# Split float32r products in place of one float32 product in the first transform step of the last two groups

## The chip, the cores and the metric

The kernel runs on one core of a Trainium2 chip. The metric is the device time of one launch in microseconds. Before the change, three runs took 2855.52, 2855.0 and 2850.59 us, a median of 2855.0.

The names of the engines: PE multiplies matrices (PEld is its loading of weights), DVE and ACT work on vectors, POOL is the fourth engine, SP issues most of the DMAs.

## The reference, cut to what matters

```python
X = np.fft.rfft(x, axis=1)                 # x: 8 batches, 3008 points, 256 channels
Yr = Xr @ w_r - Xi @ w_i + b_r
Yi = Xr @ w_i + Xi @ w_r + b_i
Yr = np.sign(Yr) * np.maximum(np.abs(Yr) - lam, 0.0)      # the same for Yi
y = np.fft.irfft(Yr + 1j * Yi, n=3008, axis=1)
gate = 1.0 / (1.0 + np.exp(-(y @ w_gate)))                # 256 -> 1536
out = (gate * (y @ w_val)) @ w_out                        # 1536 -> 256
```

3008 is 47 x 64. The forward transform is done as 47-point transforms over the rows of a batch (the "a" step), stored to DRAM, and then as 64-point transforms with twiddles (the "b" step). The changed products are those of the "a" step.

## The kernel before, in words

**Stages.** Eight batches are transformed in five groups of 1, 1, 2, 2 and 2 batches (`GROUPS`). Batches 0 and 1 and the "a" step of batches 2 and 3 are done in the first part, whose order is written by hand. From there on the main loop runs the gated feed-forward layer over columns of the output that are ready (`ffn[j]()`, 12 products of 512 columns into the banks pg and pv, and 6 into po for the unit two earlier). Beside it runs a list `side` with the transforms of the later groups: the "a" steps of group 3 (batches 4 and 5) merged with the rest of groups 1 and 2, and the "a" steps of group 4 (batches 6 and 7) merged with the rest of group 3. A unit of `side` is taken when the accumulated rate has paid its weight (the first entry of each pair); a step of "a" weighs 1.7. What is left of the program, a scheme with fewer products for the other columns, follows from about 1100 us.

**What sets the order.** Outside the parts under `manual_schedule`, the program's instructions are put in order by a scheduler that looks ahead: within each engine's queue it may put an instruction of a later unit ahead of one of an earlier unit. On the chip each engine then works through its queue in that order, and waits where an input or a buffer isn't free.

**A unit of "a"** (`step_a`, line 426) loads a tile two steps ahead (`load_a`), calls `fwd_a` (line 175) and stores the result (`store_a`). `fwd_a` makes two products of 94 x 512 elements by `fa_sb` (94 x 96) into banks named pa, straight from the loaded float32 tile `xf`, and ACT copies each bank back into `xf`. There are 2 groups of 2 batches of 8 such steps, 32 in all, with 64 products.

**A unit of the rest** (`step`, line 448) has three pieces for three different q: `fwd_b` (products pb, copy xsf, split into xsh and xsl), `mix` (18 products pm and pm3, the sums yt and ys, the soft threshold yc at lines 253 and 254, and the split into yh and yl) and `inv_b` (6 products pi, the copy vz). `inverse` adds products pia of the last inverse step. These products are float32r already, where their input is split into a high and a low part: high by high, high by low and low by high weights. pb and pia are float32.

**Buffers.** Banks pa, pb, pm, pm3, pi and pia share three PSUM buffers (`FFT_BANKS`). yt, ys and yc take turns in five buffers of the tag f2k (`NF2K`).

Of the kernel before, what the change touches and what calls it, by code (L numbers as in the profile page):

```python
# [10 lines left out]
F32R = mybir.dt.float32r  # L11
# [8 lines left out]
R2, R1 = 47, 64  # L20
NK2 = 24
NQ = 2 * NK2
# [7 lines left out]
NF2K, NR2K, NLD, NST, NBIG, NME, NVF, NVO, NHH, NSG, NYF = 5, 4, 3, 3, 5, 2, 3, 1, 3, 2, 2  # L30
# [9 lines left out]
def _r12(v):  # L40

    m, e = np.frexp(v)
    return np.ldexp(np.rint(m * 4096.0), e - 12)


def _split(v):
    hi = _r12(v)
    lo = _r12(v - hi)
    return hi.astype(np.float32), lo.astype(np.float32)


def _cs(num, den):

    num = np.asarray(num, np.int64) % den
    a = 2.0 * np.pi * num / den
    c, s = np.cos(a), np.sin(a)
    q = 4 * num
    c[(q == den) | (q == 3 * den)] = 0.0
    s[(num == 0) | (2 * num == den)] = 0.0
    return c, s  # L60


def _tables(seq):
    n2 = np.arange(R2)
    k2 = np.arange(NK2)
    c, s = _cs(n2[:, None] * k2[None, :], R2)
    fa = np.zeros((R2, 2, NK2, 2, 2))
    fb = np.zeros((NK2, 2, 2, 128))
    for j in range(2):
        fa[:, j, :, 0, j] = c  # L70
        fa[:, j, :, 1, j] = -s
        fb[:, 0, j, j:2 * R2:2] = c.T / seq
        fb[:, 1, j, j:2 * R2:2] = -s.T / seq
    fa = fa.reshape(2 * R2, 2 * NQ)
    fb = fb.reshape(2 * NQ, 128).astype(np.float32)
    n1 = np.arange(R1)
    k1 = np.arange(R1)
    mf = np.zeros((NK2, 128, 128), np.float32)
    mi = np.zeros((NK2, 128, 128), np.float32)
    mis = np.zeros((NK2, 128, 2, 128), np.float32)  # L80
    for q in range(NK2):
        k = q + R2 * k1
        c, s = _cs(n1[:, None] * k[None, :], seq)
        flip = np.where(k > seq // 2, -1.0, 1.0)
        m = np.zeros((2, R1, 2, R1))
        m[0, :, 0] = c
        m[1, :, 0] = s
        m[0, :, 1] = -s * flip
        m[1, :, 1] = c * flip
        w = np.full(R1, 2.0)  # L90
        if q == 0:
            w[k > seq // 2] = 0.0
            w[(k == 0) | (2 * k == seq)] = 1.0
        e = np.zeros((2, R1, 2, R1))
        e[0, :, 0] = (w * c).T
        e[1, :, 0] = (-w * flip * s).T
        if q:
            e[0, :, 1] = (w * s).T
            e[1, :, 1] = (w * flip * c).T
        mf[q] = m.reshape(128, 128)  # L100
        mi[q] = e.reshape(128, 128)
        mis[q, :, 0], mis[q, :, 1] = _split(e.reshape(128, 128))
    return {"mf": mf, "mi": mi, "mis": mis, "fa": fa.astype(np.float32), "fb": fb}


@with_exitstack
def tile_fft_mix_ffn(ctx: ExitStack, tc, x, w_r, w_i, b_r, b_i, w_one, w_out, mf, mi, mis, fa, fb, out):
    nc = tc.nc
    B, S, D = x.shape
    P = 128  # L110
# [11 lines left out]
    sub = nc.vector.tensor_sub  # L122
# [7 lines left out]
    cw = fft.enter_context(tc.tile_pool(name="cw", bufs=1))  # L130
    p2 = fft.enter_context(tc.tile_pool(name="p2", bufs=2))
# [4 lines left out]
    def bank(name, tag="fft", bufs=FFT_BANKS):  # L136
        return (psf if tag == "fft" else psl).tile([P, 512], F32, tag=tag, bufs=bufs, name=name)
# [6 lines left out]

    fa_sb = cw.tile([2 * R2, 2 * NQ], F32, name="fa_sb")
    nc.scalar.dma_start(fa_sb, fa)

    zd = [tc.dram_tile([NQ, R1, D], F32, name=f"zd{b}") for b in range(B)]
    vd = [tc.dram_tile([NQ, R1, D], F32, name=f"vd{b}") for b in range(B)]
# [7 lines left out]
    held = {}  # L157
# [6 lines left out]
    def load_a(b, h):  # L164
        xf = p0.tile([P, 4, D], F32, name="xf0", bufs=R1 // 8) if b == 0 else big("xf")
        for lo_, hi_ in ((0, 64), (64, 2 * R2)):
            nc.sync.dma_start(xf[lo_:hi_], xv[b, lo_:hi_, 4 * h:4 * h + 4])
        held["x", b, h] = xf

    def product_a(xi, az, copy):  # L170
        pa = bank("pa")[:2 * NQ]
        nc.tensor.matmul(pa, fa_sb, xi, start=True, stop=True)  # L172
        copy(az, pa.rearrange("p (h c) -> p h c", h=2))

    def fwd_a(b, h):

        xf = held["x", b, h]
        for i in range(2):
            at = slice(2 * i, 2 * i + 2)
            product_a(xf[:2 * R2, at], xf[:2 * NQ, at], nc.vector.tensor_copy if b < 2 and i else nc.scalar.copy)  # L180

    def store_a(b, h, queue=nc.sync):
        queue.dma_start(zv[b][:, 4 * h:4 * h + 4], held.pop(("x", b, h))[:2 * NQ])

    def load_half(b, h):
        xf = p2.tile([P, 2, D], F32, tag="ld", bufs=NLD, name="xfh")
        for lo_, hi_ in ((0, 64), (64, 2 * R2)):
            nc.sync.dma_start(xf[lo_:hi_], xv[b, lo_:hi_, 2 * h:2 * h + 2])
        held["xh", b, h] = xf
# [9 lines left out]
    def load_mf(q):  # L199
        t = p2.tile([P, 2, P], F32, name="mf_sb", bufs=NME)  # L200
        nc.sync.dma_start(t, mf[2 * q:2 * q + 2].rearrange("q p k -> p q k"))
        return t

    def load_mi(q, full):
        t = p2.tile([P, 2, 2, P], F32 if full else F32R, tag="mi_sb", bufs=NME, name="mi_sb")
        if full:
            t = t[:, :, 0]
            nc.sync.dma_start(t, mi[2 * q:2 * q + 2].rearrange("q p k -> p q k"))
        else:
            m = md[2 * q:2 * q + 2].rearrange("q p a k -> p q a k")  # L210
            if q in kept:
                nc.sync.dma_start(t.bitcast(F32), m)
            else:

                nc.gpsimd.dma_start(t, mis[2 * q:2 * q + 2].rearrange("q p a k -> p q a k"))
                nc.gpsimd.dma_start(m, t.bitcast(F32))
                kept.add(q)
        return t

    def load_b(b, q):  # L220
        zf = p2.tile([P, 2, D], F32, tag="ld", bufs=NLD, name="zf")
        nc.sync.dma_start(zf, zd[b][4 * q:4 * q + 4].rearrange("(q a) n c -> (a n) q c", q=2))
        held["z", b, q] = zf
# [88 lines left out]
    def load_v(u):  # L312
        own = 2 * UT <= u * UT < T0
        vf = p3.tile([P, 2, D], F32, tag="vo" if own else "vf", bufs=NVO if own else NVF, name="vf")[:2 * NQ]
        b, h = divmod(2 * u, H)
        nc.sync.dma_start(vf, vv[b][:, h:h + 2])
        held["v", u] = vf
# [102 lines left out]
    def fft_units(bs):  # L420

        aa = [(b, h) for b in bs for h in range(R1 // 8)]
        ms = {}
        units = []

        def step_a(i):
            if i == 0:
                for k in range(min(PRE, len(aa))):
                    load_a(*aa[k])
            if i + PRE < len(aa):  # L430
                load_a(*aa[i + PRE])
            fwd_a(*aa[i])
            store_a(*aa[i])

        def loads(q, b):
            if b == bs[0]:
                if q == 0:
                    ms[0, 0] = load_mf(0)
                if q + 1 < NP:
                    ms[q + 1, 0] = load_mf(q + 1)  # L440
                if 0 <= q - 1 < NP:
                    ms[q - 1, 1] = load_mi(q - 1, False)
            if q == 0:
                load_b(b, 0)
            if q + 1 < NP:
                load_b(b, q + 1)

        def step(q, b):
            loads(q, b)
            if q < NP:  # L450
                fwd_b(b, q, ms[q, 0], False)
            if 0 <= q - 1 < NP:
                mix(b, q - 1)
            if 0 <= q - 2 < NP:
                inv_b(b, q - 2, ms[q - 2, 1], False)

        first = [(1.7, lambda i=i: step_a(i)) for i in range(len(aa))]
        for q in range(NP + 2):
            wt = 0.9 * (q < NP) + 2.0 * (0 <= q - 1 < NP) + 0.7 * (0 <= q - 2 < NP)
            units += [(wt, lambda q=q, b=b: step(q, b)) for b in bs]  # L460
        return first, units
# [413 lines left out]
    with tc.manual_schedule():  # L875
        for u in own0:
            load_v(u)
        for f in range(NF):
            ffn[f]()
            for i in range(f * len(beside) // NF, (f + 1) * len(beside) // NF):  # L880
                if i + 2 < len(beside):
                    load_half(*beside[i + 2])
                half_a(*beside[i])
            if parts:
                load_part()
# [22 lines left out]
    n = len(a3) // 3  # L908
# [12 lines left out]
    for j in range(NF, len(ffn)):  # L921
        c, f = divmod(j, NF)
# [42 lines left out]
    with tc.manual_schedule():  # L965
        for k in range(2 * NPR * NH):
            p, e = divmod(k, 2 * NH)
# [14 lines left out]
        n = NPR * NH  # L982
# [33 lines left out]
```

## Time and profile before

| | us |
|---|---|
| median of three runs | 2855.0 |
| the profiled execution | 2855.93 |
| its span, first to last instruction | 2854.1 |
| first and last start of the changed products | 227.7 and 751.6 |
| granted TensorE clock, mean | 0.995 |

The profile's rows of groups give line, engine, operation, the names out<-in, shapes and count; then the busy time and the mean duration of one in ns; then the idle time of the engine just before these instructions and what ended it. A row of waits gives who waited for whom: total us, times, longest. A row of the timeline gives start, duration, engine, line and count; several equal instructions in a row are merged into one. A row of windows gives a stretch, its length and the busy time of PE, PEld, DVE, ACT and POOL with counts, the granted clock, the share of DMA and GB/s.

### The profile page before, as it was taken

The numbers are of one execution on the slowest core, as the hardware profiler recorded it, in microseconds if no ns is written. First come the engines' busy times: TensorE is split into PE (matmuls) and PEld (weight loads), VectorE is DVE, ScalarE is ACT, GpSimd is POOL, SyncE is SP. The second block draws the span as 40 slices with busy tenths as digits, with TensorE's granted clock in tenths as the row PEclk, the third lists the DMA queues.
The fourth block names the chain that finished last, engine by engine and source line by source line (L and its number), as shares of the span: only waits on it lengthen the run. The fifth ranks groups of instructions, "written<-read, shape, count | busy, mean of one in ns | idle before, by whom it ended". The sixth has DMA issues, their size and how long they took to land.

```text
span 2854.1 us, 38298 instructions
## 1 busy us (share of the span) xinstructions
PE 2814.8 (99%) x13892; PEld 2313.2 (81%) x13892; DVE 2087.6 (73%) x3110; ACT 1318.9 (46%) x2293; POOL 712.4 (25%) x642
## 2 busy tenths in 40 slices
PE   8899999999999999999999999999999999999999
PEld 6668888888889977888888888888888888888887
DVE  4668777667878725777777777777777777777776
ACT  4565445455455433444444444444444444444443
POOL 0111000002900001323333333333333333333321
PEclk9999999999999999999999999999999999999999
DMA  9676644655654481000000000000000000000000
GB/s 269 198 241 189 176 140 132 172 171 179 210 162 147 140 236 60 15 16 30 30 30 15 16 30 30 15 15 30 30 30 15 16 30 30 16 15 30 30 16 15
DMA packets 174509, 240.49 MB, mean 84 GB/s; under 512 B 15792, under 2 KB 126096, under 8 KB 174320
## 3 DMA queue, kind: packets, MB, share of 16 engines
q1 hardware_dynamic: 164368, 212.84, 24.5%
q0 software_dynamic: 9856, 25.17, 2.7%
q8 instruction: 110, 1.80, 0.3%
q14 instruction: 79, 0.65, 0.1%
q10 hardware_dynamic: 96, 0.04, 0.0%
HBM read 133.65 MB, written 104.33 MB: 83 GB/s over the span
## 4 chain that ended last, share of the span: by engine, by line
PE 90%; DMA 4%; DVE 3%; issue 2%; ACT 1%; SPq 0%; POOL 0%; DVEq 0%; ACTq 0%; POOLq 0%
PE pd L634 11%; PE pc L634 11%; PE pa L634 11%; PE po L606 7%; PE po L605 7%; PE po L604 7%; PE pb L634 5%; PE pm L264 5%; PE pia L333 3%; PE pb L230 3%; PE pa L172 2%; PE po L410 1%; PE po L411 1%; PE pv L387 1%; PE po L412 1%
## 5 line engine op out<-in xcount | busy, mean ns | idle before, releaser
L606 PE MATMUL po<-hl,w 128*128 128x512 f32 x912 | 362.5, 397 | 0.0
L605 PE MATMUL po<-hh,w 128*128 128x512 f32 x912 | 361.6, 397 | 0.0
L604 PE MATMUL po<-hh,w 128*128 128x512 f32 x912 | 360.9, 396 | 0.0
L693 POOL TENSOR_TENSOR c<-c,c 128x512 f32<-128x512 f32 x114 | 147.8, 1296 | 806.0 <-DVE c L689 632.2
L634 PE MATMUL pc<-s,w1h 128*128 128x512 f32 x912 | 284.1, 393 | 2.8 <-DVE v L668 2.8
L634 PE MATMUL pa<-a,w1h 128*128 128x512 f32 x912 | 284.1, 393 | 0.5 <-ACT u L660 0.5
L689 DVE TENSOR_TENSOR c<-u,pc 128x512 f32<-128x512 f32 x228 | 156.7, 687 | 114.7 <-PE pc L634 106.3
L664 DVE TENSOR_TENSOR u<-u,pb 128x512 f32<-128x512 f32 x228 | 155.3, 681 | 88.6 <-PE pb L634 62.7
L584 ACT CAST hh<-v 128x512 fp32r<-128x512 f32 x114 | 70.7, 620 | 306.3 <-DVE v L674 306.3
L606 PEld LDWEIGHTS po<-hl,w 128*128 128x128 f32 x912 | 171.5, 188 | 41.9
L604 PEld LDWEIGHTS po<-hh,w 128*128 128x128 f32 x912 | 172.0, 189 | 41.0
L634 PEld LDWEIGHTS pc<-s,w1h 128*128 128x128 f32 x912 | 170.8, 188 | 41.4 <-DVE v L668 4.1
L634 PEld LDWEIGHTS pa<-a,w1h 128*128 128x128 f32 x912 | 171.1, 188 | 41.0 <-ACT u L660 0.9
L605 PEld LDWEIGHTS po<-hh,w 128*128 128x128 f32 x912 | 171.0, 188 | 40.7
L588 POOL TENSOR_TENSOR hl<-c,hh 128x512 fp32r<-128x512 f32 x114 | 152.6, 1339 | 186.1 <-ACT hh L584 186.1
L264 PE MATMUL pm<-w_sb,xsh 128*128 128x256 f32 x1008 | 190.1, 288 | 0.3 <-DVE ys L270 0.3
L634 PE MATMUL pc<-s,w1l 128*128 128x512 f32 x456 | 177.5, 389 | 0.0
L634 PE MATMUL pa<-a,w1l 128*128 128x512 f32 x456 | 177.0, 388 | 0.0
L666 DVE TENSOR_TENSOR v<-u,pd 128x512 f32<-128x512 f32 x228 | 156.9, 688 | 24.4 <-DVE u L664 0.9
L695 DVE TENSOR_TENSOR u<-u,pd 128x512 f32<-128x512 f32 x228 | 156.8, 688 | 24.4 <-DVE c L689 0.9
L668 DVE TENSOR_TENSOR v<-v,pc 128x512 f32<-128x512 f32 x228 | 156.7, 687 | 24.4 <-DVE v L666 0.9
L660 ACT COPY u<-pa 128x512 f32<-128x512 f32 x228 | 133.7, 587 | 79.4 <-PE pa L634 79.4
(164 smaller groups left out, 6773.1 us busy)
## 6 DMA issues: line engine op xcount, KB each, us to landing
zf<-zd SPq DMA_DIRECT2D x96, 256.0 KB, 3.6
vf<-vd SPq DMA_DIRECT2D x128, 192.0 KB, 3.1
out_dram<-ot SPq DMA_DIRECT2D x94, 256.0 KB, 2.1
vd<-vz SPq DMA_DIRECT2D x84, 256.0 KB, 2.9
ypair<-yd SPq DMA_DIRECT2D x19, 1024.0 KB, 5.0
yd<-yf SPq DMA_DIRECT2D x103, 188.0 KB, 3.0
zd<-xf SPq DMA_DIRECT2D x40, 384.0 KB, 3.5
xf<-in_x_dram SPq DMA_DIRECT2D x48, 256.0 KB, 4.4
```

The costliest lines, as they stand in the source:

```text
L264: nc.tensor.matmul(o, l, r, start=(i == 0), stop=(i == len(mms) - 1))
L588: sub_(hl, h, hh)
L604: nc.tensor.matmul(o, wh, hh, start=(f == 0), stop=False)
L605: nc.tensor.matmul(o, wl, hh, start=False, stop=False)
L606: nc.tensor.matmul(o, wh, hl, start=False, stop=(f == NF - 1))
L634: nc.tensor.matmul(o, l, r, start=not more and l is wh and r is xh, stop=l is wl, skip_group_check=more)
L664: add(u, u, b)
L666: add(v, u, d)
L668: add(v, v, c)
L689: add(c12, u, c)
L693: nc.gpsimd.tensor_mul(c12, g12, c12)
L695: add(u, u, d)
```

## The change

`fwd_a_split` takes the place of `fwd_a` in `step_a`, so in groups 3 and 4 alone. For each of the two products of a step, ACT casts the input to float32r (xah), DVE subtracts it from the input (xal), and three float32r products add up in the bank: high weights by xah, high weights by xal, low weights by xah. The split weights `fas` are a new input (94 x 2 x 96), loaded on POOL's queue. xah and xal take the five buffers of the tag f2k. The weight of a step in the side list goes from 1.7 to 1.36. The first part keeps `fwd_a` and `half_a`.

```diff
     fa = fa.reshape(2 * R2, 2 * NQ)
+    fas = np.stack(_split(fa), 1)
...
+    fas_sb = cw.tile([2 * R2, 2, 2 * NQ], F32R, name="fas_sb")
...
+    def fwd_a_split(b, h):
+
+        xf = held["x", b, h]
+        for i in range(2):
+            at = slice(2 * i, 2 * i + 2)
+            hi, lo = (p2.tile([P, 2, D], F32R, tag="f2k", bufs=NF2K, name=n)[:2 * R2] for n in ("xah", "xal"))
+            nc.scalar.copy(hi, xf[:2 * R2, at])
+            sub(lo, xf[:2 * R2, at], hi)
+            pa = bank("pa")[:2 * NQ]
+            for k, (v, t) in enumerate(((0, hi), (0, lo), (1, hi))):
+                nc.tensor.matmul(pa, fas_sb[:, v], t, start=(k == 0), stop=(k == 2))
+            nc.scalar.copy(xf[:2 * NQ, at], pa.rearrange("p (h c) -> p h c", h=2))
...
-            fwd_a(*aa[i])
+            fwd_a_split(*aa[i])
             store_a(*aa[i])
...
-        first = [(1.7, lambda i=i: step_a(i)) for i in range(len(aa))]
+        first = [(1.36, lambda i=i: step_a(i)) for i in range(len(aa))]
...
         for u in own0:
             load_v(u)
+        nc.gpsimd.dma_start(fas_sb, fas)
```

The scheduler spreads the new instructions. On PE, the order of before at one step (the 15th of 32), behind a layer unit; po are the second layer's products, pa the two products of the step, pb those of the next unit:

```order
L333 MATMUL pia<-fb_sb,vf 128x94 x4
L410 MATMUL po<-hh,w_103 128x512
L411 MATMUL po<-hh,w_103 128x512
L412 MATMUL po<-hl,w_103 128x512
L410 MATMUL po<-hh,w_103 128x512
L411 MATMUL po<-hh,w_103 128x512
L412 MATMUL po<-hl,w_103 128x512
L172 MATMUL pa<-xf,fa_sb 96x512 x2
L230 MATMUL pb<-mf_sb,zf 128x128 x4
```

And on PE the 15th step of the change (its line numbers are 15 higher for what was there before); ahead of these rows stand, since the last product of the mix, 6 products pi and the other 11 products pg and pv:

```order
L402 MATMUL pv<-yth,w1l 128x512
L194 MATMUL pa<-xah,fas_sb 96x512
L425 MATMUL po<-hh,w_104 128x512
L426 MATMUL po<-hh,w_104 128x512
L427 MATMUL po<-hl,w_104 128x512
L194 MATMUL pa<-xal,fas_sb 96x512
L194 MATMUL pa<-xah,fas_sb 96x512 x2
L348 MATMUL pia<-fb_sb,vf 128x94 x4
L425 MATMUL po<-hh,w_104 128x512
L426 MATMUL po<-hh,w_104 128x512
L194 MATMUL pa<-xal,fas_sb 96x512
L194 MATMUL pa<-xah,fas_sb 96x512
```

The step that stood in one piece is taken apart: the product by xah opens the first bank, other products stand between, and the two products by xal come four and nine rows later.

On DVE, at the same step of the change, from the last sums of the mix (ys, yc) to the next unit (xsf):

```order
L286 TENSOR_TENSOR ys<-yt 64x256
L268 TENSOR_SCALAR yc<-ys 128x512
L269 TENSOR_TENSOR yc<-ys,yc 128x512
L191 TENSOR_TENSOR xal<-xf,xah 94x512
L408 TENSOR_TENSOR sg<-sg,pv 128x512
L291 TENSOR_TENSOR yl<-yc,yh 128x512
L191 TENSOR_TENSOR xal<-xf,xah 94x512
L414 TENSOR_TENSOR hl<-sg,hh 128x512
```

The first xal is put directly behind the mix's last subtraction, the second behind the layer's product sg and the mix's yl. Before, DVE had nothing of a step in its queue.

On ACT, at the same step of the change:

```order
L406 ACTIVATE sg<-pg 128x512
L190 CAST xah<-xf 94x512 x2
L290 CAST yh<-yc 128x512
L195 COPY xf<-pa 96x512
L413 CAST hh<-sg 128x512
L195 COPY xf<-pa 96x512
```

The two casts are new, between the sigmoid and the mix's cast; the two copies of pa stood there before, next to each other or not.

More of the change, by code (lines that the diff above doesn't have):

```diff
@@ L102, in _tables, with tile_fft_mix_ffn @@
         mis[q, :, 0], mis[q, :, 1] = _split(e.reshape(128, 128))
-    return {"mf": mf, "mi": mi, "mis": mis, "fa": fa.astype(np.float32), "fb": fb}
+    return {"mf": mf, "mi": mi, "mis": mis, "fas": fas, "fa": fa.astype(np.float32), "fb": fb}
 @with_exitstack
-def tile_fft_mix_ffn(ctx: ExitStack, tc, x, w_r, w_i, b_r, b_i, w_one, w_out, mf, mi, mis, fa, fb, out):
+def tile_fft_mix_ffn(ctx: ExitStack, tc, x, w_r, w_i, b_r, b_i, w_one, w_out, mf, mi, mis, fas, fa, fb, out):
     nc = tc.nc
```

## The prediction

> **What bounds the kernel now.** I read the engines' shares first, then the waits of PE (TensorE), then the stretch where the changed steps run.
>
> ```profile
> span 2854.1 us, 38298 instructions
> PE 2814.8 (99%) x13892; PEld 2313.2 (81%) x13892; DVE 2087.6 (73%) x3110; ACT 1318.9 (46%) x2293; POOL 712.4 (25%) x642
> ```
>
> PE is busy 99% of the span. A busy PE need not be a fast one, so the starts of its instructions must be read too (below). The changed products are the f32 ones of line 172 between 227 and 755 us; the groups of that stretch:
>
> ```profile
> L172 PE MATMUL pa<-xf,fa_sb 94*96 94x512 f32 x128 | 60.9, 596 | 0.0
> L173 ACT COPY xf<-pa 96x512 f32<-96x512 f32 x64 | 37.1, 582 | 16.0 <-PE pa L172 15.8
> ```
>
> There are 128 instructions for 64 products: a float32 product stands in the trace as two. 64 products are 32 steps of two. The waits of PE in the same stretch, and its windows row:
>
> ```profile
> PE pia L333 <- DMA vf<-vd: 1.5, 1, 1.5
> PE pi L301 <- ACT yh L275: 0.6, 2, 0.3
> PE pia L333 <- DVE yt L266: 0.3, 1, 0.3
> PE pm L264 <- DVE ys L270: 0.3, 1, 0.3
> ...
> 227.00:755.00 528.00, 525.08 (x3186) 443.43 (x3185) 391.37 (x675) 264.47 (x447) 71.64 (x106) 1.00 0.57 169
> ```
>
> These waits sum to 2.7 us of 528, at a granted clock of 1.00. The columns of the last row are PE, PEld, DVE, ACT and POOL: DVE is busy 391 us (74%), ACT 264 (50%). So PE sets the pace. Its work counts in full where it is taken away, and any new wait of PE counts in full too.
>
> **The saving: starts, not durations.** The mean of 596 ns per instruction overlaps with the next one, so I take the distance between starts, at one step in the PE timeline.
>
> ```profile
> 245.38 0.39 PE L410 MATMUL po<-hh,w 128*128 128x512 f32 x1
> ...
> 246.77 1.88 PE L172 MATMUL pa<-xf,fa_sb 94*96 94x512 f32 x4
> 248.49 1.06 PE L230 MATMUL pb<-mf_sb,zf 128*128 128x128 f32 x8
> ```
>
> Six float32r products of 512 columns (the row at 245.38 and the five left out) take 246.77 - 245.38 = 1.39 us, 0.232 each. The two float32 products of the step take 248.49 - 246.77 = 1.72 us, 0.86 each. Three float32r products for each are 6 x 0.232 = 1.39 us. A step saves 0.33 us, and 32 steps save **10.6 us**. The new products have 94 rows and 96 columns where these have 128; I take the same distance, since the 512 moving columns are the same.
>
> The Trainium skill ("FP8 and Floating Point Precision", section TensorE Precision Notes) says that a true FP32 product takes four passes through the array. Four passes of 0.232 would be 0.93 us per product, and the saving 64 x (0.93 - 0.70) = 14.8 us instead of 10.6. The trace has 0.86, so the measured distance is used.
>
> **What is added.** Each product needs a cast on ACT (xah) and a subtraction on DVE (xal) first. The nearest rows of the stretch:
>
> ```profile
> L276 DVE TENSOR_TENSOR yl<-yc,yh 128x512 fp32r<-128x512 f32 x54 | 38.3, 709 | 10.8 <-ACT yh L275 7.5 <-PE pg L387 2.8
> L393 DVE TENSOR_TENSOR sg<-sg,pv 128x512 f32<-128x512 f32 x52 | 35.8, 688 | 29.4 <-PE pv L387 27.5 <-ACT sg L391 1.0
> L275 ACT CAST yh<-yc 128x512 fp32r<-128x512 f32 x55 | 34.1, 620 | 48.7 <-DVE yc L254 48.6
> ```
>
> A subtraction lies between 0.69 and 0.71 us; I take 0.70. 64 of them are 45 us, and DVE goes from 391 to 436 us of some 528 (83%). 64 casts of 0.62 are 40 us, and ACT goes to 304 (58%). Neither engine becomes the bound by its sum. What counts is the moment: until now PE could start a step as soon as its input had landed; now it waits for ACT and then DVE, whose queues run in order.
>
> **When the low part is ready.** The new order puts the first xal directly behind the last subtraction of the mix (yc). So I walk one unit of before, from the start of the first inverse product after the mix (call it M = 600.00), first PE, then DVE, then ACT.
>
> ```profile
> 600.00 0.28 PE L301 MATMUL pi<-yh,mi_sb 128*128 128x256 f32 x1
> ...
> 600.72 1.03 PE L333 MATMUL pia<-fb_sb,vf 96*128 96x94 f32 x8
> 601.52 0.48 PE L385 MATMUL pg<-yth,w1h 128*128 128x512 f32 x1
> ...
> 604.40 0.39 PE L410 MATMUL po<-hh,w 128*128 128x512 f32 x1
> ```
>
> ```profile
> 599.49 0.69 DVE L266 TENSOR_TENSOR yt<-pm,bias_sb 128x512 f32<-128x512 f32 x1 [0.32 <-PE pm L264]
> ...
> 603.50 0.69 DVE L254 TENSOR_TENSOR yc<-ys,yc 128x512 f32<-128x512 f32 x1
> ```
>
> ```profile
> 603.21 0.60 ACT L391 ACTIVATE sg<-pg 128x512 f32<-128x512 f32 x1 [0.96 <-PE pg L387]
> 604.22 0.62 ACT L275 CAST yh<-yc 128x512 fp32r<-128x512 f32 x1 [0.42 <-DVE yc L254]
> ```
>
> DVE is busy without a break from 599.49 to 603.50 + 0.69 = 604.19, that is M + 4.19. ACT takes yc up at 604.22, so a hop between engines costs 0.03 us. The first xal then ends at 4.22 + 0.70 = 4.92, and PE sees it at **M + 4.95**. The cast before it is no limit: behind sg it ends some 0.65 us later, before M + 4.5.
>
> *When PE wants it.* I counted in the new order what stands between the mix and the first xal product of each of the 32 steps.
> - **11 steps**: 6 inverse products (600.72 - 600.00 = 0.72), 12 layer products (2.78), the xah product (0.23), 3 po products (0.70; in one step 2): wanted at 4.43, late by 0.52. The second xal stands behind sg and yl on DVE: 4.92 + 0.69 + 0.71 + 0.70 + 0.03 = 7.05. PE wants it at 6.25, 6.46 or 6.67 (in 3, 6 and 2 steps). The larger of the two delays is 0.80, 0.59 and 0.52 us: 2.4 + 3.5 + 1.0 = 6.9 us.
> - **4 steps** have the pia products ahead too. Without a step, the 13th layer product starts at 604.40; with the xah product ahead, xal is wanted at 4.63, late by 0.32. The second xal follows at once. 4 x 0.33 = 1.3 us.
> - **10 steps** want the first xal at 3.5 to 6.3 and have yl or sg ahead of it on DVE, or both, and hl and yl ahead of the second. The same count gives delays from 0.4 to 0.95 us, 6.2 us together.
> - **7 steps** come long after the mix, or have DVE free: nothing.
>
> Sum 14.4 us of new waits. They don't recover: PE had nothing else to wait for (2.7 us), so no other wait shrinks.
>
> **The rest.** The copies from pa (0.58 us on ACT) stay 64. The lower price of a step (1.36 for 1.7) moves side units by some 3% of their weight; the number of PE rows behind the last mix product is the same in both orders, so I take nothing. Its ends are the idle time of the next stretch, 6.8 us lost or gained:
>
> ```profile
> 755.00:1100.00 345.00, 338.24 (x2177) 301.53 (x2176) 216.83 (x365) 155.82 (x277) 34.53 (x49) 1.00 0.57 170
> ```
>
> The load of fas_sb, 72 KB, now stands first on POOL's queue, ahead of stores that come tens of us later. The nearest POOL issue:
>
> ```profile
> L215 POOL DMA_DIRECT2D mi_sb<-in_mis_dram x9 | 6.5, 717 | 29.3 <-PE pi L303 29.3
> ```
>
> Its price lies between nothing and 0.7 us while the first inputs arrive; I take nothing.
>
> **Sum.** The profiled execution took 2855.93 us (span 2854.1), 0.9 above the median of 2855.0. 2855.93 - 10.6 + 14.4 = 2859.7; against the median **2859 us**, +0.14%. About 0.2% (5.7 us) is what a measurement of this kernel can tell from no change.
>
> **Rivals.**
> - *All waits hidden, 20%.* If DVE reaches yc earlier than in the row above, xal is there in time and the saving stays whole: 2855.0 - 10.6 = 2844.4. For it: the 2.7 us of waits now. Against it: DVE's chain from 599.49 to 604.19 has hardly a gap, and PE does 4.43 us of work in its 4.95.
> - *Half hidden, 13%.* The ten steps of the third group don't wait and the second xal comes in time: 11 x 0.52 + 1.3 = 7.0 us of waits, 2851.4.
> - *DVE runs out of slack, 24%: slower.* Between two mixes DVE idles ahead of xsf and yt:
>
> ```profile
> DVE xsf L244 <- ACT xsf L242: 50.9, 46, 4.2
> ...
> DVE yt L266 <- PE pm L264: 14.4, 41, 1.1
> ...
> L244 DVE TENSOR_TENSOR xsf<-xsf 128x256 f32<-128x256 f32 x55 | 24.3, 442 | 51.1 <-ACT xsf L242 50.9
> ```
>
> That is 1.11 + 0.35 = 1.46 us per mix, hardly more than the 1.40 that a step adds. Where a unit has less than 1.40, yt starts late, and the chain to yc, the release of the mix's banks and the next low part with it. 46 of 55 units had the xsf wait; if the other 16% of the 32 steps pay the whole 1.40, it is 7 us more: 2866.
>
> **Chances.** The forecast 43% (2855 to 2863), the others as above. Faster by over 0.2%: 18%, most of the first rival. Slower by over 0.2% (above 2860.7): the last rival and a third of the forecast, 39%. Within 0.2%: 43%. The range is 2845 to 2871: it leaves out what of the first rival lies below its whole saving less 0.6 us, and a last rival of more than twice its price.
>
> **What would show it.** Right: among the waits of PE in the stretch, pa on DVE xal as the largest, some 25 times, 0.3 to 0.9 us each, 10 to 18 us together; six starts of a split step 0.23 us apart where nothing waits. Wrong: no such wait and a span some 10 us shorter; or PE waiting for DVE and ACT at pm and pb (banks) rather than at pa; or starts of the 94-row products farther apart than 0.23.

## The result and the profile after

Four runs of the changed kernel took 2869.06, 2868.24, 2874.26 and 2872.98 us, a median of **2871.0 us**; four of the kernel before on the same chip had a median of 2855.26. The ratio is **1.0055** (95% interval 1.0044 to 1.0067): 0.55% slower. The profiled execution took 2869.06 us, with a span of 2867.1, that is 13.0 above the span of before.

The head of the page of the changed kernel (span, then busy time, share and count for each engine):

```profile
span 2867.1 us, 38622 instructions
PE 2817.0 (98%) x13956; PEld 2326.4 (81%) x13956; DVE 2120.9 (74%) x3174; ACT 1349.9 (47%) x2357; POOL 713.8 (25%) x643
```

DVE gained 33 us and ACT 31; PE's busy time hardly moved. The groups of the changed kernel between 227 and 755 us, where line 194 holds the new products, 191 the subtraction and 190 the cast:

```profile
L194 PE MATMUL pa<-xah,fas_sb 94*96 94x512 f32 x125 | 46.6, 408 | 0.6 <-ACT xah L190 0.6
L191 DVE TENSOR_TENSOR xal<-xf,xah 94x512 fp32r<-94x512 f32 x62 | 43.2, 705 | 3.1 <-DMA mi_sb<-md 2.8 <-ACT xah L190 0.3
L190 ACT CAST xah<-xf 94x512 fp32r<-94x512 f32 x64 | 38.7, 614 | 2.8 <-DVE ys L286 2.0 <-PE pa L194 0.4 <-DVE yl L291 0.2
...
L194 PE MATMUL pa<-xal,fas_sb 94*96 94x512 f32 x62 | 28.0, 452 | 9.2 <-DVE xal L191 8.8
```

The casts and subtractions last what the prediction took for them (0.62 and 0.70). The waits of PE in that stretch, the first two rows of their view:

```profile
PE pa L194 <- DVE xal L191: 8.8, 16, 3.7
PE pi L316 <- ACT yh L290: 0.6, 2, 0.3
```

The wait that the prediction named is the largest, with 16 entries rather than 25 and 8.8 us rather than 10 to 18, but its longest is 3.7 us, where 0.9 was expected. The windows of the changed kernel that stand beside those shown of before:

```profile
227.00:755.00 528.00, 516.55 (x3218) 448.40 (x3216) 421.87 (x734) 292.13 (x505) 65.93 (x97) 0.99 0.56 167
755.00:1100.00 345.00, 335.91 (x2154) 300.12 (x2155) 216.14 (x365) 155.51 (x276) 40.85 (x58) 0.99 0.58 172
```

PE is idle 11.5 us of the first stretch instead of 2.9, and the clock is no longer 1.00. **Where the time went** is found by setting equal points of the two programs beside each other. First PE's timeline of before, at the first product pg of the layer's 61st unit, and at the first product of the scheme that ends the program:

```profile
683.97 0.48 PE L385 MATMUL pg<-yth,w1h 128*128 128x512 f32 x1
...
1104.99 0.62 PE L634 MATMUL pa<-a,w1h 128*128 128x512 f32 x2
```

And the same two points of the changed kernel:

```profile
680.70 0.48 PE L400 MATMUL pg<-yth,w1h 128*128 128x512 f32 x1
...
1117.29 0.63 PE L649 MATMUL pa<-a,w1h 128*128 128x512 f32 x2
```

Ahead of the first point both kernels have done 27 of the 32 steps and the same other products, and the changed one is 3.3 us *earlier*. Between the two points it loses 12.3 + 3.3 = 15.6 us, and five steps run there. Of these, 13.0 us are lost by the layer's 75th unit, the next point at which all 32 steps and the same other products are done (828.23 us in before, 837.93 in the change). The other 2.6 us are lost behind it, at waits for yf (4.6 us, 2.3 in before) and at a fall of the clock at 1079 us, not at the steps. The last two steps in PE's timeline:

```profile
736.47 0.47 PE L194 MATMUL pa<-xah,fas_sb 94*96 94x512 f32 x1 [0.41 <-ACT xah L190]
...
741.36 0.74 PE L194 MATMUL pa<-xal,fas_sb 94*96 94x512 f32 x1 [3.71 <-DVE xal L191]
...
745.73 0.63 PE L194 MATMUL pa<-xah,fas_sb 94*96 94x512 f32 x1
746.16 0.63 PE L427 MATMUL po<-hl,w 128*128 128x512 f32 x1
...
757.08 0.47 PE L194 MATMUL pa<-xal,fas_sb 94*96 94x512 f32 x1 [2.20 <-DVE xal L191]
```

Two waits of 3.71 and 2.20 us. Behind the first, two products of 512 columns start 746.16 - 745.73 = 0.43 us apart, not 0.23. The windows of the changed kernel around them show why (the columns of busy time are PE, PEld, DVE, ACT, POOL; then the granted clock):

```profile
736.00:742.00 6.00, 1.88 (x7) 1.15 (x7) 5.87 (x8) 1.65 (x3) 5.90 (x8) 0.92 0.33 131
742.00:750.00 8.00, 8.00 (x40) 7.17 (x39) 3.11 (x6) 2.75 (x5) 7.59 (x13) 0.63 0.43 129
750.00:757.00 7.00, 4.88 (x26) 3.67 (x24) 6.77 (x9) 3.76 (x6) 6.90 (x10) 1.00 0.54 192
757.00:765.00 8.00, 7.92 (x34) 7.21 (x35) 3.40 (x6) 2.52 (x5) 7.66 (x13) 0.57 0.40 128
```

After each wait the clock falls for some 7 us; in before it is 1.00 in all four stretches. The two falls cost 6 x 0.08 + 8 x 0.37 + 8 x 0.43 = 6.9 us. POOL and, at the two waits, DVE are busy throughout. So PE waited for a low part that was late, and then ran slowly.

What POOL does there is `make_t`, which neither the diff nor the prediction touched: from a certain unit of the main loop on (`c >= 5`) it forms, six sums and a split at a time, the factors tb and tr of the scheme that ends the program. It began at 656 us with one piece and went on at 681 and 691 us; from 720 to 780 us POOL is busy 57.7 of 60 us. The groups of DVE between 680 and 780 us, first of before, then of the changed kernel (yc and xal are both subtractions of 512 columns):

```profile
L254 DVE TENSOR_TENSOR yc<-ys,yc 128x512 f32<-128x512 f32 x10 | 11.1, 1110 | 0.3
```

```profile
L269 DVE TENSOR_TENSOR yc<-ys,yc 128x512 f32<-128x512 f32 x9 | 8.8, 977 | 0.3
L191 DVE TENSOR_TENSOR xal<-xf,xah 94x512 fp32r<-94x512 f32 x10 | 8.6, 879 | 0.0
```

A subtraction that took 0.69 us elsewhere (the row of 603.50 in the prediction) takes 1.11 on average in this stretch, in the kernel before as well. There little on PE hung on it: PE's waits of before in this stretch sum to 0.8 us.

### The profile page after: what moved, and what is told of

Its sections match the earlier page's. It is cut to its first block, busy times and chain, and to the rows that moved or that the text cites. A ratio compares the mean times of both kernels' runs of the same rounds, so it can differ in the third digit from the quotient of the medians.

```text
span 2867.1 us, 38622 instructions
## 1 busy us (share of the span) xinstructions
PE 2817.0 (98%) x13956; PEld 2326.4 (81%) x13956; DVE 2120.9 (74%) x3174; ACT 1349.9 (47%) x2357; POOL 713.8 (25%) x643
## 4 chain that ended last, share of the span: by engine, by line
PE 87%; DVE 6%; DMA 3%; issue 3%; ACT 1%; SPq 0%; POOL 0%; DVEq 0%; POOLq 0%; ACTq 0%
PE pd L649 11%; PE pc L649 11%; PE pa L649 11%; PE po L621 7%; PE po L620 7%; PE po L619 7%; PE pb L649 5%; PE pm L279 5%; PE pia L348 4%; PE pb L245 3%; PE pa L194 2%; PE po L425 1%; PE po L427 1%; PE po L426 1%; PE pa L174 1%
```

## The experiments

**The theories.** *Theory 1*: POOL's sums of `make_t` run beside DVE in the last five steps and stretch DVE's subtractions; the low parts come 2 to 4 us late, and the clock falls after each such wait. *Theory 2*: the split's own load on ACT and DVE makes the low parts late, and POOL only stands beside it. The expectations of e1, e3 and e5 take theory 2 in the form that the waits are spread evenly over all 32 steps, against which the equal points above already speak; e9 takes it as it stands here. *A third*: the new weight of a step, 1.36 for 1.7, puts other units into a worse place.

**1. make_t moved behind the steps (e1), and its control (e2).** The edit, in the changed kernel and in the kernel before:

```diff
-        if ts and c >= 5 and f % 2:
+        if ts and j >= 69:
             make_t(*ts.pop(0))
```

> The change, with the POOL work of make_t (sums of weights for the last part) begun at unit 69 instead of 61, behind the last split step, one call a unit. Theory 1 (the loss is made in the last four steps, where POOL works beside DVE: the subtractions stretch from 0.7 to 1.0-1.4 us, PE waits 2 to 4 us for the low part and its clock drops): the waits over 1.5 us and the drop of the granted clock at 742 and 757 us are gone, and it stands at most 3 us from e2. Theory 2 (all 32 steps wait too long, evenly): still 12 to 16 us above e2.

> The kernel before, with the same shift of make_t: the control of e1. Both theories: 2853 to 2860; what it differs from the kernel before is what the shift itself costs or brings.

Measured: e1 2869.0 us, ratio 1.0055 (1.0038 to 1.0072); e2 2854.07, ratio 1.0005 (0.9995 to 1.0014). e1 stands 14.9 us above e2, as theory 2 would have it. But it doesn't test the theories: the scheduler moved the sums forward again, and POOL's timeline of e1 begins with them at 689.53 us, ahead of the last steps:

```profile
689.53 1.42 POOL L523 TENSOR_TENSOR tb<-w1h,w1l 128x256 f32<-128x256 f32 x2 [390.76 <-DMA zd<-xf]
```

PE still waited 7.5 us for xal between 680 and 780 us, up to 3.0 at a time. An edit of the source was no edit of the queue.

**2. The same with buffers in the way (e5), and its control (e6).** Four tiny tiles of the same tag were to hold the sums back.

```diff
-        if ts and c >= 5 and f % 2:
+        if j == 70:
+            for _ in range(NBIG - 1):
+                nc.gpsimd.memset(big("pad")[:, :1, :1], 0.0)
+        if ts and j >= 70:
             make_t(*ts.pop(0))
```

> The change, with make_t's POOL work held behind the last split step by its buffers (in e1 it still began at 690 us, since the scheduler moved it up). Theory 1 (the loss is made where POOL slows DVE's subtractions and PE's clock then drops): no wait of PE for xal over 1.5 us and no drop of the clock, and -3 to +4 us against e6; the waits of the 27 earlier steps eat up their saving. Theory 2 (the loss is spread over all steps): 12 us or more above e6.

> The kernel before with make_t held back in the same way: the control of e5 and e7. 2850 to 2858 by both theories.

Measured: e5 2870.41 us, ratio 1.0065 (1.0052 to 1.0078); e6 2854.81, ratio 1.0007 (0.9998 to 1.0016). The sums began at 690 us again, PE waited 7.0 us for xal between 680 and 780 us, and the clock was 0.83 from 740 to 760. Inconclusive as well, for the same reason.

**3. make_t without its sums (e9), and its control (e10).** What moving couldn't do, leaving out did: the buffers and the store of tr stay, the sums and the split on POOL go.

```diff
-        for k, f in enumerate((f0, f1)):
-            g.tensor_add(b[:, k], w1h[:, f, i], w1l[:, f, i])
...
-        g.tensor_sub(t[:, 3], b[:, 0, 1], t[:, 1])
+        g.memset(w[:, 0, 0, :1], 0.0)
         r = p2.tile([P, 2, 4, P], F32R, tag="big", bufs=NBIG, name="tr")
-        for k in (0, 2):
-            g.tensor_copy(r[:, 0, k:k + 2], t[:, k:k + 2])
-            g.tensor_sub(r[:, 1, k:k + 2], t[:, k:k + 2], r[:, 0, k:k + 2])
+        g.memset(r.bitcast(F32), 0.0)
```

> The changed kernel, with make_t's sums and its split left out on POOL: one small memset of tb and one memset of tr stand in their place, the buffers and the store of tr stay. The seven-product scheme of the last piece so runs on zeros in t1 to t4. Theory 1 (POOL's sums beside DVE's subtractions make the low parts of the last split steps late, and the clock falls after those waits): DVE's L191 is back near 0.68 us after 690 us, no wait of the products for it over 1.5 us there, no slice of 740 to 780 us under a clock of 0.95, and the time is about 10 us below that of the change, 2859 to 2863 (what is left is the weight's 4.7 us). Theory 2 (the split's own load on ACT and DVE does it, POOL only stands beside): waits of 2 us and more for the low part stay, and the time is that of the change, 2868 to 2874. If buffers are what counts (tb and tr hold two of the five that the loads of x rotate through, and come free sooner here), the waits for the loads of x shrink and not DVE's subtractions.

> The control of the run before it: the kernel before the change, with make_t's sums and split left out in the same way. Both theories: within 3 us of the kernel before, since nothing in it waits for those sums; if it gains several us too, the run before it has to be compared with this one and not with the kernel before.

Measured: e9 **2852.04 us**, ratio 0.9995 (0.9987 to 1.0004); e10 2851.43, ratio 0.9989 (0.9980 to 0.9998). In e9, DVE's groups and the waits of PE between 680 and 780 us, and one of the two slow windows:

```profile
L269 DVE TENSOR_TENSOR yc<-ys,yc 128x512 f32<-128x512 f32 x10 | 6.9, 692 | 0.3
...
L191 DVE TENSOR_TENSOR xal<-xf,xah 94x512 fp32r<-94x512 f32 x10 | 6.6, 680 | 0.0
```

```profile
PE pa L194 <- DVE xal L191: 0.6, 3, 0.2
```

```profile
742.00:750.00 8.00, 7.82 (x45) 6.26 (x45) 6.94 (x12) 5.47 (x10) 0.00 (x0) 1.00 0.24 80
```

The same ten subtractions are back at 0.68 us, the waits at 0.6 us instead of 8.0, the clock at 1.00. In e10, the kernel before without the sums, yc is back at 0.69 us as well. The DMA engines didn't stretch it: between 680 and 780 us they are busier in e9 (0.67 of the time) than in the changed kernel (0.57). Theory 1 holds and theory 2 falls: the split's load on ACT and DVE is all there in e9. The time fell further than theory 1 said (2859 to 2863), and e10 lies 0.11% below the kernel before, so the sums cost a little there too. Against their controls, the change costs 0.06% with the sums left out (0.9995 to 0.9989, some 1.7 us by the ratios, 0.6 by the medians) and 0.55% with them. So some **14 to 15 of its 15.8 us** exist only where POOL's sums run beside the split; the intervals of the four ratios, about 0.1% to each side, leave this open by some 5 us. The equal points agree: from the 61st to the 75th unit of the layer the changed kernel loses 13.0 us on the kernel before, and e9 0.7 us on e10. The tiles tb and tr also came free sooner in e9. That the loads of x gained by it was the other reading of e9; but no product of the changed kernel waits for such a load in that stretch, and the row that moved is the subtraction.

**4. Only group 3 split (e3).** Its 16 steps are done by 497 us, before POOL begins.

```diff
-            fwd_a_split(*aa[i])
+            (fwd_a_split if bs == groups[3] else fwd_a)(*aa[i])
```

> The split for group 3 alone; group 4 keeps its float32 products. All split steps then lie ahead of the POOL work. Theory 1: -4 to +1 us against the kernel before (16 steps save 5.3 us and wait about as much). Theory 2: half of the measured loss, +8 us.

Measured: 2857.72 us, ratio 1.0023 (1.0015 to 1.0032), +5.1 us by the medians. That is above theory 1's range and below theory 2's 8 us, though the interval (4.3 to 9.1 us) doesn't exclude the latter. PE waited only 1.9 us for xal, but 2.7 us for the sums ys of the mix, a wait that the changed kernel doesn't have at that size. That led to the weight.

**5. The weight by itself (e8), and the change with the old one (e11).**

```diff
-        first = [(1.7, lambda i=i: step_a(i)) for i in range(len(aa))]
+        first = [(1.36, lambda i=i: step_a(i)) for i in range(len(aa))]
```

> The kernel before with the weight 1.36 alone, float32 products unchanged: what the pacing of the side list does by itself. The prediction took nothing for it: within 3 us of before. Theory 3 (the pacing moves units into a worse place): 4 us or more above before, which e3 would then have paid too.

> The change with the weight of a step left at 1.7. Theory 1 with the pacing as a cost of its own (the weight alone cost the kernel before 4.7 us): 2864 to 2868. The rival (the weight matters only to the kernel whose step is 1.72 us long; with the shorter step 1.36 is right): 2871 or more.

Measured: e8, the kernel before with nothing but the new weight, 2858.45 us, ratio 1.0021 (1.0011 to 1.0032), +4.7 us. In its timeline an inverse product meets a load of vf that isn't there yet, and the clock falls behind that wait too (PE's timeline, then the window):

```profile
781.69 0.71 PE L333 MATMUL pia<-fb_sb,vf 96*128 96x94 f32 x2 [2.38 <-DMA vf<-vd]
```

```profile
780.00:800.00 20.00, 18.31 (x104) 17.60 (x105) 8.26 (x16) 7.50 (x14) 2.08 (x4) 0.74 0.50 161
```

20 x 0.26 = 5.2 us of clock. So the weight costs e8 and, since it waits for ys in the same places, probably e3: with e8 as its control (1.0023 to 1.0021) the split of group 3 costs next to nothing. But it isn't a price that adds. e11, the change with the old weight, took 2867.69 us. That lies in the range expected for a price that adds (2864 to 2868), but the kernel before took 2853.3 us on that chip, and the ratio, 1.0053 (1.0040 to 1.0065), is that of the change. There the weight moves the units, and the waits beside POOL stay (9.8 us for xal, up to 3.9 at a time). The third theory explains no share of the result that these intervals can tell from nothing.

**6. Low parts made early (e4).** The casts and subtractions of a step are written one side unit ahead of its products; the second half's parts get a buffer of the larger tag.

```diff
+    def split_a(b, h):
...
+        s = p2.tile([P, 4, D], F32R, tag="big", bufs=NBIG, name="xas")[:2 * R2]
...
+            nc.scalar.copy(hi, xf[:2 * R2, at])
+            sub(lo, xf[:2 * R2, at], hi)
+            held["xa", b, h, i] = hi, lo
...
             acc -= side[0][0]
+            if side[0][1] not in ahead_of and len(side) > 1 and ("x", *ahead_of.get(side[1][1], ())) in held:
+                split_a(*ahead_of[side[1][1]])
             side.pop(0)[1]()
```

> The change, with the casts and subtractions of a step written one side unit earlier (the second half's parts in a buffer of the tag big, so that they fit), so that PE should find both low parts ready; POOL's work stays where it is. Theory 1 and the prediction's own sum: without waits the saving of 10.6 us lands, 2843 to 2849, and no drop of the clock in the last steps. Theory 2 in the form that float32r products are no cheaper here: 2855 or more. If DVE and ACT are simply overloaded by 45 and 40 us of work: above 2860 with the waits moved to pm and pb.

Measured: 2854.21 us, ratio 1.0003 (0.9995 to 1.0012), outside what was expected (2843 to 2849). The waits for xal are down to 0.8 us between 680 and 780 us, but a new one stands in their place, in the waits of PE and of ACT there:

```profile
PE pia L362 <- ACT vz L334: 5.4, 1, 5.4
```

```profile
ACT xas L195 <- POOL tr L550: 6.3, 2, 5.6
```

The cast into xas waits for a buffer of the tag that `make_t` uses too; the copy vz stands behind it in ACT's queue, and PE waits for vz. The clock is 0.86 from 720 to 740 us.

**7. Both (e7), and with the old weight (e12).** e4 with `make_t` held back as in e5; here the sums began at 709 us.

> e4 (casts and subtractions one unit earlier) with make_t held back as in e5. Theory 1: e4's one wait of 5.4 us (ACT's cast waited for a buffer that POOL's make_t held) is gone too, and the whole saving lands: 8 to 11 us below e6. If products of split input save nothing here: at e6.

> The version that beat both kernels (the split written one side unit ahead, make_t from unit 70 on), with the weight left at 1.7. If the weight's cost adds to the rest wherever the low parts are ready: 4 us below its 2844.6, some 2840. If the cost of the weight was only where its side units fell beside make_t: 2843 to 2846.

Measured: e7 **2844.57 us**, ratio 0.9977 (0.9967 to 0.9987); it is 10.2 us below its control e6 (8.6 us by the ratios). It beats both kernels. A step in its PE timeline (line 208 holds the products):

```profile
568.05 0.40 PE L208 MATMUL pa<-xah,fas_sb 94*96 94x512 f32 x1
568.29 0.39 PE L208 MATMUL pa<-xal,fas_sb 94*96 94x512 f32 x1
568.52 0.40 PE L208 MATMUL pa<-xah,fas_sb 94*96 94x512 f32 x1
568.75 0.86 PE L208 MATMUL pa<-xas,fas_sb 94*96 94x512 f32 x3
569.45 0.80 PE L362 MATMUL pia<-fb_sb,vf 96*128 96x94 f32 x6
```

Six products take 569.45 - 568.05 = 1.40 us, no wait for xal is left between 227 and 780 us, and the clock is 1.00 from 680 to 800. e12 took 2850.18 us, ratio 0.9984 (0.9975 to 0.9993), above both ranges that were expected. Its interval and that of e7 overlap, so the old weight is not shown to be worse there, and it is no better. It has two waits and a slow stretch of its own (last section).

## Why the prediction was right and wrong

The time, 2871.0 us, lies at the very end of the range (2845 to 2871), not at the forecast of 2859; of the three outcomes it was slower, which had 39%. The mechanism was right, and one term was missing.

- **The saving, 10.6 us: right.** Six products take 1.40 us where nothing waits (e7; the prediction had 1.39). From the layer's 14th unit, ahead of the first step, to its 61st, behind the 27th, the profiled execution of e7 gains 8.5 us on that of e6, where 27 x 0.33 = 8.9 was forecast. That the medians of the two lie 10.2 us apart, so close to 10.6, is in part luck: by the ratios it is 8.6 us, and e12 with the other weight is only 4.6 us below e6. The four passes that the Trainium skill ("FP8 and Floating Point Precision", section TensorE Precision Notes) states for a true FP32 product gave a saving of 14.8 us, 12.5 of it in 27 steps, only because each pass was taken to last as long as a float32r product (0.232 us). That saving isn't borne out; but the 0.86 us of the trace is also four times 0.215, and no run shows how long one pass lasts.
- **The waits of the ordinary steps: right in place, too large.** For the first 27 steps the terms of the prediction give 27 x 0.33 = 8.9 us saved and, of 14.4 us of waits, 27/32, 12.2: 3.3 us later. The trace has 3.3 us earlier. But most of that is a stall in the profiled execution of before, which isn't a matter of the steps (its timeline of PE, then a window):

```profile
317.88 1.10 PE L333 MATMUL pia<-fb_sb,vf 96*128 96x94 f32 x8 [1.51 <-DMA vf<-vd]
```

```profile
318.90:322.20 3.30, 3.30 (x17) 3.30 (x17) 0.42 (x1) 1.06 (x2) 0.00 (x0) 0.50 0.34 81
```

  The wait is 1.51 us, and the clock then stands at 0.50 for 3.4 us, which costs 1.7. The changed kernel waits 0.31 us for this load and has no fall there, nor has the profiled execution of e10. Without these 2.9 us the 27 steps gain 0.4, so their waits cost some 8.5 us rather than 12.2. In e9 against e10, without POOL's sums, all 32 steps together come out at nothing (0.1 us earlier): the waits there eat up the whole saving. In the step shown next, the first xal is late as forecast, and the second is in time. The changed kernel on PE, and DVE beside it:

```profile
606.53 0.39 PE L194 MATMUL pa<-xah,fas_sb 94*96 94x512 f32 x1
607.18 0.47 PE L194 MATMUL pa<-xal,fas_sb 94*96 94x512 f32 x1 [0.27 <-DVE xal L191]
...
609.21 0.47 PE L194 MATMUL pa<-xal,fas_sb 94*96 94x512 f32 x1
```

```profile
605.85 0.69 DVE L408 TENSOR_TENSOR sg<-sg,pv 128x512 f32<-128x512 f32 x1
606.45 0.68 DVE L191 TENSOR_TENSOR xal<-xf,xah 94x512 fp32r<-94x512 f32 x1
607.05 0.68 DVE L291 TENSOR_TENSOR yl<-yc,yh 128x512 fp32r<-128x512 f32 x1
```

  DVE's subtractions start 0.60 us apart where they last 0.69: they overlap by 0.09, as PE's products do. The prediction took starts on PE, but added whole durations on DVE, so that each low part came 0.1 us too late for each instruction ahead of it. In the row of 607.18, PE loses 607.18 - 606.53 - 0.23 = 0.42 us; the wait listed is 0.27, since the product before is counted as busy past the moment at which the next could start. That is why waits as listed (3.0 us for xal before 680) are less than what they cost. And "no other wait shrinks" was too strict, as the wait for vf shows.
- **The step that failed: "a subtraction lies between 0.69 and 0.71 us; I take 0.70", for all 32 steps.** In the last five it takes 0.88, and the chain ahead of it is stretched as well. The duration came from groups over 227 to 755 us and from a unit at 600 us; no row of the prediction is of the stretch from 680 us on alone, where POOL is busy. It held the answer: yc at 1.11 us. What this cost is the missing term: the waits of 8.4 us for xal and xah between 680 and 780 us and the 6.9 us of clock are 15.3 us, where the changed kernel lost 13.0 net from the 61st to the 75th unit, 14.7 with the five steps' saving of 1.7.
- **The clock: not thought of.** The prediction held that a wait of PE counts in full. Behind the waits of 3.71 and 2.20 us the clock cost about 3.4 us more each.
- **The weight, taken at nothing: right here, with luck.** Alone in the kernel before it costs 4.7 us (e8), within the ends of 6.8 that were given for it; in the change, 1.7 and 1.36 give the same ratio, within intervals of 0.12% (e11).
- **The rivals.** "DVE runs out of slack", at 2866, has the right engine and sign, but it isn't the cause: DVE idles as much ahead of xsf as before (51.5 us of waits there from 227 to 755, 50.9 before), and with the same load on DVE e9 doesn't lose it. "All waits hidden", at 2844.4, is not what the change does, but what e7 comes near to, with the low parts made ahead of time. That e7's 2844.57 agrees so closely is chance: the kernel before took 2853.74 us on that chip.

## What to carry to other kernels

Read an engine's durations in every stretch in which the new instructions will run, and note which other engine is busy there: a mean over the whole stage hid a factor of 1.6. Where the matrix engine is the bound, a new operand that another engine has to make should be made a unit ahead, and out of the way of other work that slows that engine or holds its buffers (e4 alone gained nothing, e7 did); put directly in front of its use, beside POOL's sums, it turned a saving of 10 us into a loss of 16. And before an experiment that moves work is believed, look in the trace whether the work moved.

## What the runs showed of the hardware

**DVE beside POOL.** Beside POOL's sums, DVE's yc and xal took 0.94 to 1.52 us at the two long waits instead of 0.68 or 0.69, but not all of its instructions were stretched. At the first long wait of the changed kernel, in DVE's timeline:

```profile
739.94 1.36 DVE L191 TENSOR_TENSOR xal<-xf,xah 94x512 fp32r<-94x512 f32 x1
741.33 0.69 DVE L408 TENSOR_TENSOR sg<-sg,pv 128x512 f32<-128x512 f32 x1
```

The product sg, which reads one operand from a PSUM bank, kept its 0.69 us. The Trainium skill ("SBUF — State Buffer", section "SBUF: two separate sides") says that DVE and GpSimd (POOL) share one pair of ports, that an instruction of DVE in a mode that uses two ports, or one with two SBUF inputs beside one of GpSimd that reads SBUF, and one of GpSimd lock each other out of it, and that the loser blocks. The rows agree: xal reads xf and xah, both in SBUF, and was stretched; with memsets in place of the sums (e9) it was not. So do the groups of 680 to 780 us: the three that read a PSUM bank and one operand in SBUF have the same means in the changed kernel and in e9 (sg 0.69, yt 0.69, the first ys 0.42 us), while those with two operands in SBUF are longer beside the sums (hl 0.87 to 0.69, xsl 1.16 to 0.96, the second ys 0.59 to 0.42 us). The first half of yc, with one operand in SBUF, went from 0.44 to 0.75 us as well; no run here shows whether it used such a mode.

**The clock after short waits.** In the changed kernel both falls were to half:

```profile
741.10:747.90 6.80, 6.54 (x23) 5.56 (x24) 3.05 (x5) 2.16 (x4) 6.62 (x11) 0.50 0.30 103
758.20:764.90 6.70, 6.70 (x29) 6.16 (x28) 2.24 (x4) 2.14 (x5) 6.52 (x11) 0.50 0.47 148
```

That is 6.8 us each, so 3.4 us lost, whether the wait was 3.71 or 2.20 us. Behind 2.38 us in e8 the clock stood at 0.50 for 10.2 us, around the 5.4 us in e4 for 6.8, and behind 1.51 us in before for 3.4: the length of the fall doesn't follow that of the wait. In e12 it fell to half behind two waits of under 1 us each. PE's timeline of e12, and its windows of 2 us:

```profile
761.34 0.39 PE L330 MATMUL pi<-yh,mi_sb 128*128 128x256 f32 x1 [0.86 <-ACT yf L379]
...
764.22 0.55 PE L330 MATMUL pi<-yh,mi_sb 128*128 128x256 f32 x1 [0.67 <-PE pia L362]
```

```profile
760.00:762.00 2.00, 1.14 (x10) 0.94 (x9) 2.00 (x4) 1.19 (x3) 2.00 (x4) 1.00 0.09 32
762.00:764.00 2.00, 1.45 (x11) 1.08 (x9) 1.87 (x4) 0.96 (x2) 2.00 (x4) 0.93 0.50 108
764.00:766.00 2.00, 1.78 (x8) 1.81 (x9) 1.90 (x4) 0.22 (x2) 1.90 (x4) 0.50 1.04 369
```

PE was idle 0.86 + 0.55 us of these first 4 us, and the clock stood at 0.50 until 770. Other waits had no such effect: 1.00 us at 474 us of the changed kernel (clock 1.00 from 440 to 560), 1.75 us at 771 us of e2 (1.00 from 770 to 780), 1.89 and 1.92 us at 787 and 1067 us of e3 (1.00 in the 10 us behind each). The Trainium skill ("TensorE: Matmul & The Clock Gate", section "HAM oscillation — how this bites in real kernels") gives as its rule no idle gaps of PE over about 3.4 us; here gaps well under that were enough. So a wait of 1.5 us brought a fall and one of 1.9 us did not; what decides between them was not tried.
